# Nested seven-product T1 in the third GLU pass, projection banks seeded by ScalarE, and other stages for the down weights' sums and the k tiles

## The chip, the cores and the metric

The kernel runs on one core of a Trainium2 chip. Its time is the device time of one execution in microseconds; the median of three runs is given.

## The reference

One layer: layer norm, a hedgehog linear attention, a gated linear unit (GLU) on the same normalized input, and their product added to the input. x is 2048 rows of 1024, F is 3584; all data are fp32.

```python
xn = layernorm(x)                       # [2048, 1024]
q, k, v = split(xn @ wqkv)              # three [1024, 1024] products, 32 heads of 32
pq, pk = q @ w_phi, k @ w_phi           # per head
phi_q = concat(softmax(pq), softmax(-pq)); phi_k likewise
s = (phi_q (phi_k^T v)) / (phi_q phi_k^T 1 + 1e-6) @ wo
g = sigmoid(xn @ w_gate) * (xn @ w_up)  # [2048, 3584], here called h
out = x + s * silu(g @ w_down)
```

## The kernel before

**One product.** Every fp32 operand is split into a rounded part hi (a ScalarE cast, L133) and the rest lo (a VectorE subtraction, L134). `mm3` then issues three matmuls into one PSUM bank: hi·hi (L142), hi·lo (L143), lo·hi (L144), each 128x128 by 128x512. Seven block products take the place of eight: the large products go by a Strassen-Winograd scheme over 2x2 blocks, with operand sums made by POOL (GpSimd) and kept in DRAM. The seven are named B11, B21, T2, T3, T4, T1 and B22. B11 and B21 need no sums of weights; T2, T3 and T4 build on B11's result, T1 and B22 on what T2 and T3 left.

**Stages, in TensorE's order** (the list `ops`): the projections V, K, Q of the first half of the rows; GLU pass 0 (B11 and B21 for 14 pairs f of weight tiles); the projections of the second half; GLU pass 1 (T2, T3, T4 for each f); GLU pass 2, the *third pass* (T1 and B22 for each f); the down product (`dsteps`, 112 steps); then the attention's end and the output projection. In a GLU product, a tile f has four banks: gate and up weights (s) by two column halves of the rows (th), bank 2s+th, 12 matmuls each. Pass 1 keeps the banks after B11, T2 and T3 in DRAM (`keep_bank`, m_d), and pass 2 loads them again (`fetch`).

**h in the third pass.** `h_added` adds a bank to the fetched tile on VectorE (L1302), applies the sigmoid on ScalarE for the gate's two banks (L1304), and multiplies on POOL (L1306) for the up's two. `h_out` makes the sums of four h tiles on POOL (L1276 to L1279) and stores seven kinds of h for the down stage.

**Weights.** A ring of eight slots (`w`, `NW = 8`) holds split weights. `prep` makes the next item whenever slots are free: it takes a raw buffer loaded by `glu_load`, casts, subtracts, and gives the buffer back to `raw_free`. `tick` counts steps of the program (four per GLU product); `later(n, f)` runs f after n ticks, and such work is put behind the last matmul issued. All data transfers are issued on the SP queue.

**Sums of weights.** `glu_group` makes the sums of the gate and up weights on POOL in pass 1, for f = 2 to 12 (`FLY`). `wd_sums` makes the sums of the down weights, in 14 sets: four loads of 256 KB, four POOL subtractions of 128x512 (L789 to L792), four stores of 256 KB. In this kernel all 14 sets run in the third pass. `k_steps` and `k_end` handle the k tiles of the attention: nine in the second projections (`EARLY`), the others in pass 1, one each 6.5 ticks; the second `k_end` (transposes L678) falls into the third pass.

**Projections.** `proj_out` evacuates a bank after each product: B11 and B21 by ScalarE copies, T2, T3, T4, T1 and B22 by VectorE additions (L541) of the bank and a tile in SBUF. Products in `opening` (B11, T2, T3, T1) start a new bank.

**The way into the down stage.** `down_prep` loads and splits a weight tile and two h tiles for a later down step; it needs slots from `wfree` and `hfree`. Four slots (16 to 19) go to `wfree` after T1 of f = 12, that is 144 matmuls ahead of the first down product.

Of the kernel before, what the change touches and what calls it, by code (L numbers as in the profile page):

```python
# [18 lines left out]
P = 128  # L19
# [8 lines left out]
HB = 512  # L28
# [21 lines left out]
def hedgehog_glu_kernel(  # L50
# [62 lines left out]
    EARLY = 9  # L113
# [279 lines left out]
    ops += [("glu", p, f, i) for p in (1, 2) for f in range(NJ) for i in PASSES[p]]  # L393
    items = []
    for n, op in enumerate(ops):
        items += [(n, 2), (n, 2)] if op[0] == "proj" else [(n, 1), (n, 1)]
# [8 lines left out]
    raw_free, spare, groups, made_sums = deque(), [], deque((f, s) for f in FLY for s in range(2)), {}  # L405
# [30 lines left out]
    def glu_group():  # L436
# [3 lines left out]
        f, s = groups.popleft()  # L440
        a11, a12, a21, a22, s1 = bs = [raw_free.popleft() for _ in range(5)]
# [17 lines left out]
        if not groups:  # L459
            kept = [b for b in raw_free if not any(b is o for o in spare)]  # L460
            raw_free.clear()
            raw_free.extend(kept)

# [22 lines left out]
    def prep():  # L486
# [7 lines left out]
        if kind == "glu":  # L494
# [9 lines left out]
            glu_load(n + 1)  # L504
        flow["item"] += 1
        flow["made"] += size
        if kind == "proj":
# [19 lines left out]
    def proj_out(c, which, i, u, b, held=None):  # L527
# [255 lines left out]
    def wd_sums(j, b):  # L783
# [16 lines left out]
        later(4, sums)  # L800
        later(7, keep)
# [439 lines left out]
    def fetch(f):  # L1241
        if f == NJ or f in fetched:
            return
        if phase == 1:
            fetched[f] = [None, None, m1[4 * (f % 2):4 * (f % 2) + 4] if f else halves(48, 49)]
            for b, o in enumerate(fetched[f][2]):
                nc.sync.dma_start(o, m_d[0, f, b])
            return
        fetched[f] = {}
        for m in (2, 1):  # L1250
            fetched[f][m] = [uvfree.popleft() for _ in range(4)]
            for b, o in enumerate(fetched[f][m]):
# [71 lines left out]
    def begin_pass(p):  # L1324
# [12 lines left out]
        elif p == 1:  # L1337
            gates_r.items = halves(45, 46)
# [8 lines left out]
        else:  # L1347
            for n in range(NJ):
                queue2(3 + 8 * n if n < 3 else 26 + 13 * (n - 3) // 2, wd_sums, n,
                       halves(*((43, 44), (53, 54))[n % 2 if n > 2 else 0]))  # L1350

    phase = 0
    for n, (kind, c, what, i) in enumerate(ops):
# [3 lines left out]
        if kind == "proj":  # L1357
# [5 lines left out]
            for u in range(4):  # L1363
                if i in opening:
                    pbank[u] = pmm.next()
                us = slice(u * P, (u + 1) * P)
                for k in range(4):
                    mm3(pbank[u], (xo[:, k, 0, us], xo[:, k, 1, us]), pair(ws[k]),
                        i in opening and k == 0, k == 3, skip_group_check=True)
# [26 lines left out]
        phase, f = c, what  # L1396
# [330 lines left out]
```

## Time and profile before

| | |
|---|---|
| median of 3 runs | 2376.79 us (2374.76 to 2378.82) |
| profiled execution: its time, its span | 2374.87 us, 2373.1 us |
| busy share of the span | PE 99%, DVE (VectorE) 68%, ACT (ScalarE) 45%, POOL 40% |
| matrix matmuls L142, L143, L144 | 390, 389, 389 ns each, pipelined |
| third pass, 1308.6 to 1617.0 us | 308.4 us, DMA share 0.92 |
| down stage, 1617.0 to 2160.4 us | 543.4 us, DMA share 0.70 |

A group of instructions is given as line, engine, operation, output <- input, shape, count, then busy time in us and the mean of one in ns, then the engine's idle time just before them and what ended it. A row of windows gives the stretch, its length, the busy us of PE, PEld (weight loads), DVE, ACT and POOL with counts, the granted clock of TensorE, the DMA engines' busy share, and GB/s.

### The profile page before, as it was taken

The numbers are of one execution on the slowest core, as the hardware profiler recorded it, in microseconds if no ns is written. First come the engines' busy times: TensorE is split into PE (matmuls) and PEld (weight loads), VectorE is DVE, ScalarE is ACT, GpSimd is POOL, SyncE is SP. The second block draws the span as 40 slices with busy tenths as digits, with TensorE's granted clock in tenths as the row PEclk, the third lists the DMA queues.
The fourth block names the chain that finished last, engine by engine and source line by source line (L and its number), as shares of the span: only waits on it lengthen the run. The fifth ranks groups of instructions, "written<-read, shape, count | busy, mean of one in ns | idle before, by whom it ended". The sixth has DMA issues, their size and how long they took to land.

```text
span 2373.1 us, 32026 instructions
## 1 busy us (share of the span) xinstructions
PE 2360.2 (99%) x10972; PEld 1967.2 (83%) x10972; DVE 1610.1 (68%) x2103; ACT 1060.4 (45%) x1603; POOL 954.5 (40%) x617
## 2 busy tenths in 40 slices
PE   9999999999999999999999999999999999999999
PEld 8887888888888888888888888888888888888887
DVE  8635776674677947567766533345888998877776
ACT  7333454464333545565555422223443334355553
POOL 0323237711131045445410687853423334324566
PEclk9999999999999999999999999999999999999999
DMA  8799989975687776677756999977676766876665
GB/s 295 259 317 354 373 316 376 388 266 175 201 278 257 269 279 232 229 245 247 250 184 199 344 396 364 355 251 246 208 233 230 239 209 210 287 272 221 205 208 177
DMA packets 287732, 631.45 MB, mean 266 GB/s; under 512 B 36688, under 2 KB 36944, under 8 KB 282960
## 3 DMA queue, kind: packets, MB, share of 16 engines
q1 hardware_dynamic: 287568, 629.40, 76.1%
q8 instruction: 86, 1.41, 0.2%
q14 instruction: 78, 0.64, 0.1%
HBM read 376.31 MB, written 252.97 MB: 265 GB/s over the span
## 4 chain that ended last, share of the span: by engine, by line
PE 90%; DMA 4%; DVE 3%; POOL 1%; issue 1%; ACT 1%; SPq 0%; DVEq 0%; ACTq 0%; POOLq 0%
PE bank L142 28%; PE bank L143 28%; PE bank L144 28%; PE bank L642 1%; PE bank L932 1%; PE bank L908 1%; DMA wf_d<-fc 1%; DVE w L134 1%; DMA qkv_d<-fc 1%; PE bank L1182 1%; PE bank L366 1%; DMA fa<-wf_d 1%; DVE x L134 0%; DMA g_d<-fc 0%; DMA fc<-wo 0%
## 5 line engine op out<-in xcount | busy, mean ns | idle before, releaser
L142 PE MATMUL bank<-x,w 128*128 128x512 f32 x2352 | 915.7, 390 | 1.6 <-DVE fc L1496 1.6
L143 PE MATMUL bank<-x,w 128*128 128x512 f32 x2352 | 915.5, 389 | 0.0
L144 PE MATMUL bank<-x,w 128*128 128x512 f32 x2352 | 914.1, 389 | 0.7 <-DVE w L134 0.7
L134 DVE TENSOR_TENSOR w<-fa,w 128x512 fp32r<-128x512 f32 (+1 forms) x437 | 406.5, 935 | 216.9 <-ACT w L133 201.0
L133 ACT CAST w<-fa 128x512 fp32r<-128x512 f32 (+1 forms) x437 | 298.2, 685 | 552.4 <-PE bank L143 380.2
L142 PEld LDWEIGHTS bank<-x,w 128*128 128x128 f32 x2352 | 441.6, 188 | 92.8 <-DVE fc L1496 2.0
L144 PEld LDWEIGHTS bank<-x,w 128*128 128x128 f32 x2352 | 441.5, 188 | 92.6 <-DVE w L134 1.1
L143 PEld LDWEIGHTS bank<-x,w 128*128 128x128 f32 x2352 | 441.6, 188 | 90.7
L142 PE MATMUL bank<-w,x 128*128 128x512 f32 x708 | 278.2, 393 | 1.8 <-DVE fb L541 1.6
L143 PE MATMUL bank<-w,x 128*128 128x512 f32 x708 | 276.3, 390 | 0.2 <-DVE w L1118 0.2
L144 PE MATMUL bank<-w,x 128*128 128x512 f32 x708 | 276.0, 390 | 0.0
L142 PEld LDWEIGHTS bank<-w,x 128*128 128x128 f32 x708 | 133.0, 188 | 29.9 <-issue 1.6
L144 PEld LDWEIGHTS bank<-w,x 128*128 128x128 f32 x708 | 132.9, 188 | 28.1 <-DVE x L1108 0.3
L143 PEld LDWEIGHTS bank<-w,x 128*128 128x128 f32 x708 | 133.1, 188 | 26.4 <-DVE w L1118 0.6
L864 POOL TENSOR_TENSOR fc<-fc 128x1024 f32<-128x1024 f32 x32 | 81.6, 2549 | 180.1 <-ACT fc L584 129.7
L1261 ACT COPY fc<-bank 128x512 f32<-128x512 f32 x168 | 97.5, 584 | 102.9 <-PE bank L144 67.4
L1302 DVE TENSOR_TENSOR x<-x,bank 128x512 f32<-128x512 f32 x80 | 54.8, 687 | 117.1 <-PE bank L144 108.4
L134 DVE TENSOR_TENSOR x<-fa,x 128x512 fp32r<-128x512 f32 x112 | 112.8, 1007 | 13.7 <-ACT x L133 13.6
L876 POOL TENSOR_TENSOR fc<-fc,sa 128x1024 f32<-128x1024 f32 x32 | 70.0, 2187 | 89.7 <-DVE sa L873 89.7
L133 ACT CAST x<-fa 128x512 fp32r<-128x512 f32 x112 | 69.2, 618 | 47.8 <-DMA fa<-wd_d 27.3
L134 DVE TENSOR_TENSOR p<-fc,p 128x512 fp32r<-128x512 f32 (+1 forms) x65 | 54.1, 843 | 53.1 <-ACT p L133 52.6
L541 DVE TENSOR_TENSOR fc<-fc,bank 128x512 f32<-128x512 f32 x72 | 48.7, 681 | 42.9 <-PE bank L144 29.7
(311 smaller groups left out, 3153.2 us busy)
## 6 DMA issues: line engine op xcount, KB each, us to landing
m_d<-fc SPq DMA_DIRECT2D x168, 256.0 KB, 4.1
fa<-h_d SPq DMA_DIRECT2D x84, 512.0 KB, 4.2
x<-m_d SPq DMA_DIRECT2D x132, 256.0 KB, 5.1
fa<-wf_d SPq DMA_DIRECT2D x32, 1024.0 KB, 6.2
h_d<-fc SPq DMA_DIRECT2D x100, 256.0 KB, 5.1
fc<-e_d SPq DMA_DIRECT2D x48, 512.0 KB, 4.8
fc<-qkv_d SPq DMA_DIRECT2D x80, 256.0 KB, 4.2
fa<-wg_d SPq DMA_DIRECT2D x68, 256.0 KB, 5.1
```

The costliest lines, as they stand in the source:

```text
L133: nc.scalar.copy(o[0], src)
L134: i = nc.vector.tensor_sub(o[1], src, o[0].bitcast(F32))
L142: nc.tensor.matmul(o, a[0], b[0], start=first, stop=False, **kw)
L143: nc.tensor.matmul(o, a[0], b[1], start=False, stop=False, **kw)
L144: last_mm[:] = [nc.tensor.matmul(o, a[1], b[0], start=False, stop=last, **kw).ins]
L366: nc.tensor.matmul(ps[:, gs], r[:, gs], bd[:, 4 * f + g], start=True, stop=True)
L541: last_dve[:] = [nc.vector.tensor_add(y, x, b).ins]
L642: nc.tensor.matmul(kvb[g // 2][:, g % 2 * 256:g % 2 * 256 + 256], v[:, g].rearrange("p a f -> p (a f)"), ph[:, g].rearrange("p a f -> p (a ...
L864: nc.gpsimd.tensor_mul(ez, e, zb)
L876: nc.gpsimd.tensor_mul(e3, e3, r2[:, :, None].to_broadcast([P, 32, DH]))
L1261: nc.scalar.copy(o, banks[b])
L1302: last_dve[:] = [nc.vector.tensor_add(us[b], us[b], banks[b]).ins]
```

## The change

**Nested products.** For f = 2 to 13 in the third pass, T1 is itself made by seven products of halved blocks. `nest(n, f)` makes T1 of f+1 that way (seven products of six matmuls, 42 in place of 48) and B22 of f as before (`plain(q)`, 48 matmuls). The seven go through banks a, b, c, g (4 to 7): B11 into a, copied to b by ScalarE; T2 on top in b, copied to c; T1 into g; B21 on top in a; T3 on top in c, copied to a; T4 on top in a; B22 on top in g. `result` adds a bank to the fetched tile on VectorE (L1473) and copies it by ScalarE into bank q (L1474), where the matmuls of plain(q) then accumulate. `added` copies g to SBUF and adds it to c and to b. Each nest has six weight items: two loaded pairs of tiles are turned by four POOL sums of 128x256 (`nest_load`) into five and a half casts and subtractions. The rows' side (`x_nest_load`, `x_nest_sums`, `x_nest_split`) is made once, ahead of and at the start of the third pass.

**Projections.** Outside the first eight products, T2 and T3 accumulate in B21's bank, seeded by a ScalarE copy of the kept tile, and T2, T3 and T4 are evacuated by ScalarE copies; T1 and B22 stay VectorE additions.

**Down weights' sums.** Seven of the 14 sets move into pass 1 (between the groups of f = 4 to 10, with four raw buffers for eight ticks each), two stay in the third pass, five go to down steps 1 to 25 (`wd_steps`).

**k tiles.** Eleven in the second projections, the others one each 6 ticks, so that both `k_end` fall into pass 1.

**The way into the down stage.** Slots 16 to 19 go to `wfree` after the last nest, 48 matmuls ahead of the end of the pass.

The core of the diff:

```diff
-    EARLY = 9
+    EARLY = 11
     def tick():
             glu_group()
+            nest_load()
-    ops += [("glu", p, f, i) for p in (1, 2) for f in range(NJ) for i in PASSES[p]]
+    ops += [("glu", 1, f, i) for f in range(NJ) for i in PASSES[1]]
+    ops += [("glu", 2, 0, T1), ("glu", 2, 0, B22), ("glu", 2, 1, T1)]
+    ops += [("nest", 2, f, B22) for f in range(1, NJ - 1)] + [("glu", 2, NJ - 1, B22)]
+    WD_B, WD_C = range(7), range(7, 9)
+    for f in FLY:
+        groups.extend((f, s) for s in range(2))
+        if 0 <= f - 4 < len(WD_B):
+            groups.append((WD_B[f - 4], None))
+    def wd_group(j):
+        bs = [raw_free.popleft() for _ in range(4)]
+        wd_sums(j, bs)
...
+        later(8, free)
+    def nest_load():
+        if not nests or len(raw_free) < 6 or ops.index(("glu", 2, 1, T1)) not in wraw:
+            return
+        k = nests.popleft()
+        ra, rb, rc, rd, gate, up = [raw_free.popleft() for _ in range(6)]
+        for s, o in enumerate((ra, rb)):
+            nc.sync.dma_start(o, wg_d[summed.index(T1), k + 1, :, s * HB:(s + 1) * HB])
+        for s, o in enumerate((gate, up)):
+            last_load[:] = [nc.sync.dma_start(o, wg_d[summed.index(B22), k, :, s * HB:(s + 1) * HB]).ins]
+        def sums():
+            nc.gpsimd.tensor_add(rc[:, hi], rb[:, lo], rb[:, hi])
+            nc.gpsimd.tensor_sub(rb[:, lo], ra[:, lo], rb[:, lo])
+            nc.gpsimd.tensor_sub(rc[:, lo], rc[:, hi], ra[:, lo])
+            nc.gpsimd.tensor_sub(rd[:, lo], ra[:, hi], rc[:, lo])
+            nested[k] = rc, ra, gate, rb, rd, up
+        later(4, sums)
     proj_out:
         (B21)
+            if held is None:
+                nc.scalar.copy(b, u1p[u])
+        elif held is None and i in (T2, T3):
+            nc.scalar.copy((u1p if i == T2 else u2p)[u], b)
+        elif held is None and i == T4:
+            y = yp.next()
+            nc.scalar.copy(y, b)
+            store(0, 1, y)
     begin_pass:
-                at += 6.5
+                at += 6
         else:
-            for n in range(NJ):
-                queue2(3 + 8 * n if n < 3 else 26 + 13 * (n - 3) // 2, wd_sums, n, ...)
+            later(3, raw_free.extend, spare)
+            for n, j in enumerate(WD_C):
+                queue2(20 + 8 * n, wd_sums, j, halves(53, 54))
+    def nest(n, f):
+        def result(q, ps):
+            nc.vector.tensor_add(va[q], va[q], ps)
+            nc.scalar.copy(banks[q], ps)
+            if q < 2:
+                nc.scalar.activation(va[q], va[q], AF.Sigmoid)
+        def added(o, n):
+            x = slots[38][:, n]
+            nc.scalar.copy(x, g)
+            nc.vector.tensor_add(o, o, x)
+        product(B11, a, True)
+        nc.scalar.copy(b, a)
+        plain(0)
+        product(T2, b, False)
+        nc.scalar.copy(c, b)
+        product(T1, g, True)
+        product(B21, a, False)
+        result(0, a)
+        plain(1)
+        product(T3, c, False)
+        nc.scalar.copy(a, c)
+        added(c, 0)
+        plain(2)
+        product(T4, a, False)
+        result(2, a)
+        gated(0)
+        product(B22, g, False)
+        added(b, 1)
+        plain(3)
+        result(3, c)
+        result(1, b)
+        gated(1)
     main loop:
+        if kind == "nest":
+            nest(n, f)
+            if f == NJ - 2:
+                wfree.extend(range(16, 20))
+            tick()
+            continue
-        elif phase == 2 and f == NJ - 2 and i == T1:
-            wfree.extend(range(16, 20))
+        elif (phase, f, i) == (2, 1, T1):
+            x_nest_split(T1)
     down stage:
+        if n in wd_late:
+            wd_steps(n)
```

(`tick` and `used` calls inside `nest` are left out here.) TensorE's row at the seam between the two products of one f in the third pass, before; x0 and x2 are the split rows, w the ring of split weights:

```order
L144 MATMUL bank3_104<-x0_4_9231,w_0_94 128x512
L142 MATMUL bank0_101<-x2_5_9285,w_0_94 128x512
L143 MATMUL bank0_101<-x2_5_9285,w_0_94 128x512
L144 MATMUL bank0_101<-x2_5_9285,w_0_94 128x512
L142 MATMUL bank0_101<-x2_5_9285,w_0_94 128x512
```

T1's last bank is followed by B22's first; between two uses of a bank lie 36 matmuls of the others. The same engine after, in the middle of the nests, from T4's last matmul (rows p) on:

```order
L144 MATMUL bank4_105<-p_2_9774,w_0_94 128x512
L142 MATMUL bank7_108<-x0_4_9420,w_0_94 128x512
L143 MATMUL bank7_108<-x0_4_9420,w_0_94 128x512
L144 MATMUL bank7_108<-x0_4_9420,w_0_94 128x512
L142 MATMUL bank7_108<-x0_4_9420,w_0_94 128x512
L143 MATMUL bank7_108<-x0_4_9420,w_0_94 128x512
L144 MATMUL bank7_108<-x0_4_9420,w_0_94 128x512
L142 MATMUL bank3_104<-x6_5_9526,w_0_94 128x512
L143 MATMUL bank3_104<-x6_5_9526,w_0_94 128x512
L142 MATMUL bank4_105<-x1_4_9336,w_0_94 128x512
L143 MATMUL bank4_105<-x1_4_9336,w_0_94 128x512
L144 MATMUL bank4_105<-x1_4_9336,w_0_94 128x512
```

Bank 4 closes with T4 and is opened again by the next nest's B11 (x1) eight matmuls later. ScalarE in the third pass before; fa are raw buffers, x3, x5 and fc hold fetched tiles:

```order
L1304 ACTIVATE x5_3_9410<-x5_3_9410 128x512
L133 CAST w_0_94<-fa_0_97 128x512
L1304 ACTIVATE x3_4_9409<-x3_4_9409 128x512
L133 CAST w_0_94<-fa_0_97 128x512
L1304 ACTIVATE x3_4_9409<-x3_4_9409 128x512
L133 CAST w_0_94<-fa_0_97 128x512
L1304 ACTIVATE fc_0_100<-fc_0_100 128x512
```

It casts and applies sigmoids by turns, and touches no bank. ScalarE after, from the last evacuation of one nest through most of the next; L1492, L1496 and L1507 are the copies to b, c and a:

```order
L1474 COPY bank2_103<-bank4_105 128x512
L1480 COPY p2_2_9775<-bank7_108 128x512
L1492 COPY bank5_106<-bank4_105 128x512
L133 CAST w_0_94<-fa_0_97 128x512 x3
L1496 COPY bank6_107<-bank5_106 128x512
L133 CAST w_0_94<-fa_0_97 128x512
L1474 COPY bank0_101<-bank4_105 128x512
L1476 ACTIVATE x3_4_9582<-x3_4_9582 128x512
L1474 COPY bank1_102<-bank5_106 128x512
L1476 ACTIVATE x3_4_9582<-x3_4_9582 128x512
L1507 COPY bank4_105<-bank6_107 128x512
L1480 COPY p2_2_9775<-bank7_108 128x512
```

Nine copies from or into banks now stand between the casts, three of them (to b, c and a) between two products of the same nest, and the three casts of one group stand ahead of the copy to c.

More of the change, by code (lines that the diff above doesn't have):

```diff
@@ L504, in prep @@
             glu_load(n + 1)
+        if kind == "nest" and what not in nested:
+            return False
         flow["item"] += 1
         flow["made"] += size
+        if kind == "nest":
+            s = len(ready[n])
+            src, cols = nested[what][s], slice(0, 256 if s == 4 else HB)
+            split(cut(pair(w), cols), src[:, cols])
+            release(src)
+            ready[n].append(w)
+            return True
         if kind == "proj":
@@ L799, in wd_sums @@
             nc.sync.dma_start(b, wd_block(i, j))
-        later(4, sums)
-        later(7, keep)
+        return sums, keep
+    def wd_sums(j, b):
+        for n, f in zip((4, 7), wd_parts(j, b)):
+            later(n, f)
     def down_prep():
```

129 lines of the change are left out of this document (108 added, 21 removed).

## The prediction

> **What bounds the kernel now.** I read the page's engines and its chain first, then TensorE's (PE's) waits, then windows by stage.
>
> ```profile
> PE 2360.2 (99%) x10972; PEld 1967.2 (83%) x10972; DVE 1610.1 (68%) x2103; ACT 1060.4 (45%) x1603; POOL 954.5 (40%) x617
> PE 90%; DMA 4%; DVE 3%; POOL 1%; issue 1%; ACT 1%; SPq 0%; DVEq 0%; ACTq 0%; POOLq 0%
> ...
> PE bank L142 <- DVE fb L541: 1.6, 3, 0.8
> PE bank L142 <- DVE fc L1496: 1.6, 1, 1.6
> ...
> PE bank L908 <- DMA fc<-e_d: 1.1, 1, 1.1
> PE bank L678 <- issue: 0.8, 1, 0.8
> ```
>
> PE is busy for 2360 of 2373 us and makes up 90% of the chain; its longest wait is 1.6 us. So the time is a count of matmuls times their spacing, and a saved matmul is worth its spacing as long as what feeds PE keeps pace. The stages (length, then busy PE, PEld, DVE, ACT and POOL, clock, DMA share, GB/s):
>
> ```profile
> 590.80:828.10 237.30, 237.30 (x1081) 197.80 (x1080) 183.12 (x209) 97.48 (x114) 36.79 (x23) 1.00 0.74 249
> 828.10:1308.60 480.50, 480.50 (x2205) 400.92 (x2204) 309.53 (x342) 265.79 (x401) 179.94 (x115) 1.00 0.69 234
> 1308.60:1617.00 308.40, 307.64 (x1366) 254.72 (x1365) 131.88 (x188) 80.64 (x136) 228.57 (x167) 1.00 0.92 335
> 1400.00:1600.00 200.00, 200.00 (x885) 165.58 (x884) 81.39 (x115) 47.96 (x77) 154.63 (x113) 1.00 0.92 334
> 1617.00:1753.00 136.00, 136.00 (x602) 112.61 (x601) 106.79 (x152) 53.02 (x87) 48.06 (x22) 1.00 0.68 231
> 1753.00:2000.00 247.00, 247.00 (x1091) 204.55 (x1090) 224.16 (x330) 98.87 (x160) 88.83 (x39) 1.00 0.68 227
> ```
>
> These are the second projections, pass 1, the third pass, its middle, and two parts of the down stage. PE never rests in them, and the granted clock is 1.00 throughout. In the third pass VectorE (DVE) and ScalarE (ACT) are idle for over half the time; DMA is what is full there (0.92). In the down stage DVE is the second engine: 79%, then 91%.
>
> **The gain.** The middle of the third pass gives the spacing: 200 us / 885 = 0.226 us. A tile of the third pass has 96 matmuls, 48 of T1 and 48 of B22; in a nest T1 has seven products of six, 42. Twelve tiles save 72 matmuls, 72 x 0.226 = 16.3 us, and a tile goes from 21.7 to 90 x 0.226 = 20.3 us, if PE never waits. No other part of the change removes a matmul; all else can only cost, or free a wait that PE has now (the rows above: 1.6 + 0.8 us at most).
>
> **The nests.** The three places where one could wait are priced from these rows: a last matmul with the DVE addition and ACT operation that follow it, ACT and DVE work by kind, POOL's, and the time of loads from issue to landing.
>
> ```profile
> 1426.36 0.39 PE L144 MATMUL bank<-x,w 128*128 128x512 f32 x1
> 1426.79 0.69 DVE L1302 TENSOR_TENSOR fc<-fc,bank 128x512 f32<-128x512 f32 x1 [2.03 <-PE bank L144]
> 1427.51 0.63 ACT L1304 ACTIVATE fc<-fc 128x512 f32<-128x512 f32 x1 [0.28 <-DVE fc L1302]
> ...
> L133 ACT CAST w<-fa 128x512 fp32r<-128x512 f32 x57 | 35.4, 621 | 119.7 <-PE bank L143 97.4 <-issue 6.8 <-PE bank L144 4.2
> L134 DVE TENSOR_TENSOR w<-fa,w 128x512 fp32r<-128x512 f32 x57 | 48.6, 853 | 8.9 <-ACT w L133 8.8
> L1257 ACT COPY bank<-x x52: 578/591/615, 853.4 to 1275.5; 128x512 f32<-128x512 f32 x52
> L789 POOL TENSOR_TENSOR fb<-fb 128x512 f32<-128x512 f32 x8 | 10.4, 1295 | 36.5 <-DMA fb<-w_down 36.5
> L792 POOL TENSOR_TENSOR fc<-fc 128x512 f32<-128x512 f32 x6 | 8.7, 1453 | 0.0
> L1306 POOL TENSOR_TENSOR x<-x 128x512 f32<-128x512 f32 x22 | 31.1, 1419 | 16.2 <-DVE x L1302 16.2
> fa<-wg_d SPq DMA_DIRECT2D x43, 256.0 KB, 5.1
> ```
>
> *Throughput first.* A nest gives ACT six casts less a half (5.5 x 0.62), nine copies (9 x 0.59) and four sigmoids (4 x 0.63): 11.2 us of 20.3. DVE gets 5.5 subtractions (0.85) and ten additions (0.69): 11.6 us. POOL gets four products (1.42), four half-width sums (about 0.7, half of 1.3 to 1.45) and four sums of h (1.4): 14 us. None is full. DMA is relieved: 12 of the 14 sets of down-weight sums leave the stage, each 8 transfers of 256 KB, which is 25 MB of the 103 MB (335 GB/s x 308.4 us) that the stage moves. So only latency in the loop can bite.
>
> *Place 1, T4 to the next B11.* Both use bank a (bank 4), and eight matmuls lie between, so nine spacings, 2.03 us. In that time DVE must start after the last matmul (+0.43, from the first two rows), ACT's copy follows its start by 0.72 and takes 0.59, and some 0.05 passes on release: 1.80 us. It fits by 0.2 us if ACT is free. The copies to b, c and a have twelve matmuls or more to hide them.
>
> *Place 2, the loop through the weights.* A nest may load only when six raw buffers are free. Counted from T4's last matmul: the last cast before it starts at +0.4, behind a sigmoid; DVE's subtraction releases the buffer at +1.9; the load lands 5.1 later, +7.0; three half-width sums on POOL, +9.1; three casts follow, and queued behind the first of them on ACT stand the copy to c, another cast and the seed of bank 0, which is done at +13.6. PE arrives at plain(0) 61 spacings after, +13.8. So the loop closes with 0.2 us to spare, and a nest takes the larger of 20.34 and 20.17 + (landing - 5.1).
>
> *Place 3, the last product of B22*, whose first matmuls need a cast made after T4's fifth: some 0.5 us of slack.
>
> If no place ever waits, the price is 0; if half of the nests lose 1 us in one of them, 6. I take 1.5, nearer to the lower end, since the landing is 5.1 with a DMA share of 0.92 and that share falls.
>
> One rule of the Trainium skill speaks against the change. "TensorE: Matmul & The Clock Gate", section "A second HAM failure mode: psum-queue depth-cycling", says that cycling through banks with small idles between groups makes the clock switch between half and full speed. The traced down stage changes its bank every three matmuls and keeps 1.00, so I add nothing; by the rule the nests' clock would drop, which is a rival below.
>
> **Rows for the nests.** The four sums of two column halves of T1's rows: 8 POOL subtractions, 8 casts and subtractions, four loads of 512 KB near the seam of pass 1 and the third pass. 8 x 0.62 on ACT and 8 x 0.85 on DVE lie beside 20 us of a tile's matmuls. 0 to 2 us (a late first split, as half of the work): I take 0.5.
>
> **Projections.** These rows price them:
>
> ```profile
> L541 DVE TENSOR_TENSOR fc<-fc,bank x72: 628/680/689, 56.8 to 817.7; 128x512 f32<-128x512 f32 x72
> ...
> ACT p L133 <- DMA fc<-wo: 24.7, 8, 8.1
> ```
>
> For each of the five later projections 12 DVE additions (0.68) turn into copies of 0.59 on ACT, and four seeds are added there. PE comes back to a bank after 36 matmuls, 8.1 us, and copy and seed need 0.43 + 2 x 0.59 = 1.6. What could break it is ACT being held: it waited up to 8.1 us for wo's rows in the first projections, and copies now queue behind such a cast: 8.1 + 1.6 - 8.1 = 1.6 us, two or three times. From -1.6 (PE's waits on L541 go) to +4; I take 0.
>
> **Pass 1.** Seven sets put 28 POOL subtractions (1.3 to 1.45 each, 39 us) beside 180 us of 480, and 56 transfers of 256 KB (14.7 MB, at 335 GB/s 44 us) on the SP queue ahead of later loads, with DMA at 0.69. Four raw buffers are away for eight ticks, seven times; casts then run closer behind POOL's sums. Two k tiles more run in the projections. The wait of 0.8 at L678 may move or go. From -0.9 to +3; I take 0.
>
> **Into the down stage.** The first down product's operands could be split from 144 matmuls (32.5 us) ahead, now from 48 (10.8 us). The chain for the first is a load of about 5.1, three casts (1.9) and a last subtraction (0.85), 7.9 us, and a step of 24 matmuls is 5.4 us, above three casts or three subtractions (2.6). So it is ready before, if SP's queue isn't held; late by a landing costs 5. I take 1.5 of 0 to 5.
>
> **Sums in the down stage.** Twenty POOL subtractions (20 x 1.3 to 1.45 = 26 to 29 us) and 40 transfers come within steps 1 to 25, about 135 us, where DVE splits run:
>
> ```profile
> L134 DVE TENSOR_TENSOR w<-fa,w x140: 628/683/2627, 1622.4 to 1999.4; 128x512 fp32r<-128x512 f32 x140
> L134 DVE TENSOR_TENSOR x<-fa,x x69: 627/680/2889, 1624.7 to 1995.2; 128x512 fp32r<-128x512 f32 x69
> ```
>
> The median split takes 0.68, but up to 2.6 or 2.9 us. In the third pass, with POOL busy for 229 of 308 us, the same operation averages 0.85: 57 x 0.17 = 9.7 us lost, so 28 us more of POOL cost 28 x 9.7 / 229 = 1.2 us of DVE time. The other end is that DVE stands still for all of it, 28 us, against its idle 136 - 106.8 = 29.2 us in the first window and 22.8 in the next. Taken: 1 us, of 0 to 8.
>
> The Trainium skill's "SBUF — State Buffer", section "🔬 SBUF: two separate sides", takes that other end: an operation of DVE with both inputs in SBUF and one of GpSimd lock each other out for the whole instruction. By the longest split above (2.89) the trace bears it out for single instructions, by the mean of 0.85 not for the sum.
>
> **The sum.** -16.3 + 1.5 + 0.5 + 0 + 0 + 1.5 + 1 = -11.8 us. From the profiled execution's 2374.87 that is 2363.1; the median of the three runs lies 1.9 us above it, so the forecast is 2365.0. A difference of 0.2%, 4.75 us, is about what a measurement of this kernel can tell from no change: below 2372.0 counts as faster, above 2381.5 as slower.
>
> **Rivals.**
> *The down stage eats the gain.* If POOL's sums hold DVE for their full length, DVE's need in the first window is 106.8 + 28 = 135 of 136 us; the lead with which splits run ahead isn't rebuilt, and in the second window (91%) PE waits. If a fifth to a half of the 28 us reaches PE, 6 to 14 us come back: -11.8 - 1 + 6 to 14 from the median gives 2370 to 2378. For it: the 2.9 us. Against: DVE isn't over full even then. 0.13.
> *Slower: the nest's loop closes through the load.* A transfer of 256 KB takes 0.78 us at 335 GB/s; three more ahead of it in the queue (a fetch of four tiles, or four stores of h) make the landing 7.5 in place of 5.1. Then a nest takes 20.17 + 2.4 = 22.57, 2.2 us over PE's own, and 12 x 2.2 = 26.8: -16.3 + 26.8 + 3 = +13.5, about 2390. It outweighs the gain from a landing of about 6.4 on. For it: 0.2 us of slack, a release, a load, POOL, ACT and DVE in one chain, and in-order ACT with the seed behind the cast. Against: 5.1 is the median in a fuller queue. 0.15.
> *The clock drops in the nests,* by the many short accumulations: at half the rate 12 x 20.3 = 244 us more, 2610. No row shows a clock under 1.00. 0.02.
> *The nests don't save what they should,* since matmuls of six per bank run less tightly: at 0.240 spacing, 1080 x 0.014 = 15 us are lost and the time is unchanged, 2377 to 2380. The down stage's three per bank run at 247 / 1091 = 0.226, which speaks against it. 0.02.
> The forecast keeps 0.68.
>
> **How the numbers follow.** The forecast's own range: gains of PE's present waits (-2.5) and all costs at zero give -16.3 - 2.5 + 1.9 from 2374.87, 2358.0; costs at half their upper ends (the upper ends of 6, 2, 4, 3, 5 and 8 us don't meet), 14, give 2374.5. To hold 0.8 it takes in most of the down rival, to 2377. Faster: 0.67 of the forecast and 0.06 of the down rival, 0.73; the same: the rest of both and the loose spacing, 0.10; slower: the loop, the clock, 0.17.
>
> **What would show it.** Right: records of L142, L143 and L144 fall by 24 each; the third pass lasts about 293 us at a spacing of 0.226; PE has no wait over 0.5 us on an ACT copy or a cast within it; wg_d loads land in about 5 us or less; splits in the down stage stay near a median of 0.68. Wrong: a regular wait of 1 to 2 us per nest on plain(0)'s seed (the loop), waits of bank a on ACT at each T4 (place 1), DVE subtractions at 2 us and waits on w in 1650 to 1900 us (the down stage), or a clock under 1.00.

## The result, and the profile after

The changed kernel takes 2417.57 us (median; 2413.48 to 2420.85) against 2376.48 us: 1.0171 times the time before, 95% interval 1.0151 to 1.0192. That is slower by 41 us, where 12 us less were forecast. The profiled execution's span went from 2373.1 to 2418.3 us. The page of the changed kernel, its engines and its costliest group (count, busy us, mean ns, then the idle time before it):

```profile
PE 2364.4 (98%) x10900; PEld 1961.7 (81%) x10900; DVE 1668.7 (69%) x2099; ACT 1158.1 (48%) x1817; POOL 1019.9 (42%) x673
...
L142 PE MATMUL bank<-x,w 128*128 128x512 f32 x2304 | 900.6, 393 | 43.4 <-ACT fc L1323 19.8
```

The 72 matmuls are gone (10972 to 10900), but TensorE's idle time before L142's matmuls rose from 1.6 to 43.4 us. What it waited for (us in total, times, longest):

```profile
PE bank L142 <- ACT fc L1323: 19.8, 8, 5.8
PE bank L142 <- ACT bank L1474: 10.9, 6, 2.6
PE bank L142 <- DVE fc L1667: 5.8, 1, 5.8
PE bank L142 <- ACT bank L1319: 3.3, 3, 2.8
PE bank L142 <- DVE x L1364: 2.8, 1, 2.8
```

L1323 is `keep_bank`'s copy and L1319 the seed, both of pass 1; L1474 is the seed of plain(q) in the nests, L1364 the addition in `h_added`; L1667 is the evacuation of B21 in the down stage. Windows by stage of the changed kernel: projections and pass 0 (to the last addition of a projection), pass 1 (to the first addition in `h_added`), third pass (to the last of these), the down stage to the first sigmoid there (or its table load), and the rest:

```profile
0.00:831.00 831.00, 826.62 (x3887) 690.93 (x3888) 546.75 (x664) 429.16 (x604) 231.80 (x157) 1.00 0.83 295
831.00:1352.70 521.70, 498.56 (x2247) 411.81 (x2246) 326.07 (x343) 258.83 (x409) 234.21 (x158) 0.99 0.73 249
1352.70:1657.00 304.30, 290.38 (x1239) 235.46 (x1238) 170.05 (x223) 139.92 (x253) 211.17 (x164) 0.98 0.74 250
1657.00:1811.60 154.60, 151.11 (x666) 124.44 (x664) 126.73 (x165) 56.75 (x96) 76.52 (x40) 1.00 0.81 287
1811.60:2418.30 606.70, 597.73 (x2867) 499.10 (x2867) 499.11 (x708) 273.49 (x458) 266.18 (x156) 0.99 0.67 227
```

Cut in the same way, the kernel before has 830.9, 487.6, 298.7, 147.9 and 608.0 us. So the projections cost nothing (+0.1), pass 1 costs 34.1, the third pass 5.6 in place of a gain of 16.3, the start of the down stage 6.7, and the rest gains 1.3: together 45.2.

**The granted clock fell as well.** Two-microsecond windows around one wait in the nests:

```profile
1440.00:1442.00 2.00, 1.94 (x9) 1.09 (x7) 2.00 (x3) 1.03 (x2) 2.00 (x2) 1.00 0.90 289
1442.00:1444.00 2.00, 0.19 (x1) 0.00 (x0) 2.00 (x3) 0.00 (x0) 1.92 (x2) 1.00 0.15 39
1444.00:1446.00 2.00, 1.21 (x4) 0.98 (x5) 1.34 (x3) 1.75 (x4) 1.84 (x3) 0.82 0.95 293
1446.00:1448.00 2.00, 2.00 (x7) 1.52 (x6) 0.96 (x2) 1.23 (x3) 1.24 (x1) 0.50 1.02 360
1448.00:1450.00 2.00, 2.00 (x9) 1.63 (x8) 0.98 (x2) 0.90 (x2) 1.29 (x1) 0.82 0.93 240
```

TensorE stood for 2.6 us, took up work at full clock, and then had half the clock for some 3.4 us (0.7, 2.0 and 0.7 by the last three rows). Over the whole trace, spacings between the starts of matmuls above 0.6 us, less 0.227 each, sum to 50.1 us (6.5 before), and spacings of 0.3 to 0.6 us, where the reduced clock shows, less 0.227 each, to 28.6 us (11.2 before): 43.6 + 17.4 = 61 us lost. Less the 16.3 gained that is 44.7, against a difference of 45.2.

### The profile page after: what moved, and what is told of

It reads as the page before. It is cut to its first block, busy times and chain, and to the rows that moved or that the text cites. A ratio compares the mean times of both kernels' runs of the same rounds, so it can differ in the third digit from the quotient of the medians.

```text
span 2418.3 us, 32136 instructions
## 1 busy us (share of the span) xinstructions
PE 2364.4 (98%) x10900; PEld 1961.7 (81%) x10900; DVE 1668.7 (69%) x2099; ACT 1158.1 (48%) x1817; POOL 1019.9 (42%) x673
## 5 line engine op out<-in xcount | busy, mean ns | idle before, releaser
L142 PE MATMUL bank<-x,w 128*128 128x512 f32 x2304 | 900.6, 393 | 43.4 <-ACT fc L1323 19.8
L143 PE MATMUL bank<-x,w 128*128 128x512 f32 x2304 | 902.9, 392 | 1.1 <-DVE x L134 1.1
L144 PE MATMUL bank<-x,w 128*128 128x512 f32 x2304 | 900.2, 392 | 0.0
L134 DVE TENSOR_TENSOR w<-fa,w 128x512 fp32r<-128x512 f32 (+2 forms) x453 | 449.7, 1000 | 279.8 <-ACT w L133 256.1
L142 PEld LDWEIGHTS bank<-x,w 128*128 128x128 f32 x2304 | 435.9, 189 | 144.0 <-ACT fc L1323 23.2
L144 PEld LDWEIGHTS bank<-x,w 128*128 128x128 f32 x2304 | 435.8, 189 | 91.7 <-DVE w L134 0.4
L143 PEld LDWEIGHTS bank<-x,w 128*128 128x128 f32 x2304 | 435.8, 189 | 90.3 <-DVE x L134 1.5
L133 ACT CAST w<-fa 128x512 fp32r<-128x512 f32 (+2 forms) x453 | 303.2, 677 | 380.7 <-PE bank L143 257.6
L142 PE MATMUL bank<-w,x 128*128 128x512 f32 x708 | 277.8, 393 | 0.4 <-DVE fb L593 0.4
L142 PEld LDWEIGHTS bank<-w,x 128*128 128x128 f32 x708 | 133.1, 188 | 27.6 <-DVE fb L593 1.0
L1323 ACT COPY fc<-bank 128x512 f32<-128x512 f32 x168 | 96.6, 585 | 102.7 <-PE bank L144 52.9
L134 DVE TENSOR_TENSOR x<-fa,x 128x512 fp32r<-128x512 f32 x112 | 118.5, 1059 | 20.9 <-ACT x L133 20.7
L644 ACT ACTIVATE fc<-fc 128x1024 f32<-128x1024 f32 x48 | 50.9, 1060 | 91.9 <-DVE fc L641 78.1
L134 DVE TENSOR_TENSOR p<-fc,p 128x512 fp32r<-128x512 f32 (+1 forms) x67 | 63.5, 955 | 28.8 <-ACT p L133 28.4
L1009 POOL TENSOR_TENSOR fc<-fc 128x512 f32<-128x512 f32 x32 | 49.3, 1539 | 53.8 <-DVE fb L1020 19.9
```

The source lines that it names most:

```text
L133: nc.scalar.copy(o[0], src)
L134: i = nc.vector.tensor_sub(o[1], src, o[0].bitcast(F32))
L142: nc.tensor.matmul(o, a[0], b[0], start=first, stop=False, **kw)
L143: nc.tensor.matmul(o, a[0], b[1], start=False, stop=False, **kw)
L144: last_mm[:] = [nc.tensor.matmul(o, a[1], b[0], start=False, stop=last, **kw).ins]
L644: nc.scalar.activation(e, e, AF.Exp)
```

## The experiments

A run without interval is one profiled execution, read by stage. All are edits of the changed kernel. Single executions whose text of a stage is the same differ: the projections and pass 0 take 828.4 to 836.8 us, pass 1 with its sets 520.0 to 526.1, the third pass with two sets and eight buffers 299.9 to 304.3. Smaller differences in a stage tell nothing. Stages in us, as cut above:

| run | proj., pass 0 | pass 1 | third | to B21's end | rest | span |
|---|---|---|---|---|---|---|
| before | 830.9 | 487.6 | 298.7 | 147.9 | 608.0 | 2373.1 |
| after | 831.0 | 521.7 | 304.3 | 154.6 | 606.7 | 2418.3 |
| sets_p3 | 832.0 | 495.7 | 313.0 | 152.3 | 607.0 | 2400.0 |
| sets_dma_only | 836.8 | 520.0 | 302.5 | 155.0 | 607.2 | 2421.6 |
| hold_p1 | 831.4 | 492.8 | 311.0 | 152.0 | 605.7 | 2392.8 |
| loads_p1 | 832.7 | 511.1 | 313.9 | 152.2 | 606.2 | 2416.1 |
| stores_p1 | 832.7 | 497.2 | 312.2 | 153.3 | 605.9 | 2401.3 |
| idle_p1 | 868.8 | 495.2 | 312.8 | 152.2 | 605.3 | 2434.3 |
| k_13_65 | 832.8 | 520.8 | 300.1 | 151.1 | 607.3 | 2412.2 |
| sets_p0 | 847.1 | 495.6 | 299.9 | 152.6 | 605.8 | 2401.0 |
| no_nest | 828.8 | 529.4 | 294.8 | 147.9 | 607.2 | 2408.1 |
| nest_12raw | 830.7 | 523.6 | 289.1 | 154.4 | 607.1 | 2404.9 |
| down_lead | 834.9 | 526.1 | 303.7 | 152.2 | 606.2 | 2423.1 |
| down_p3 | 828.4 | 524.1 | 312.6 | 146.4 | 606.2 | 2417.6 |
| best1 | 846.3 | 487.4 | 286.4 | 152.0 | 605.9 | 2378.1 |
| best2 | 833.5 | 488.3 | 295.8 | 153.7 | 607.3 | 2378.6 |
| best3 | 831.5 | 488.2 | 300.1 | 156.1 | 604.9 | 2380.7 |
| best4 | 841.6 | 489.4 | 287.0 | 153.0 | 605.2 | 2376.3 |
| best5 | 839.1 | 488.2 | 293.0 | 152.8 | 604.9 | 2378.1 |
| best6 | 831.4 | 488.5 | 293.0 | 153.5 | 605.5 | 2371.8 |

**Pass 1: sets or k tiles?** From the time lines of POOL, ScalarE and VectorE of the changed kernel around the longest wait (TensorE stands from 1133.7 to 1139.4), then ScalarE's waits in the whole pass:

```profile
1122.41 1.61 POOL L458 TENSOR_TENSOR fa<-fb,fb 128x512 f32<-128x512 f32 x1 [8.18 <-DMA fb<-w_gu]
...
1126.78 0.62 ACT L133 CAST w<-fa 128x512 fp32r<-128x512 f32 x1 [2.68 <-POOL fa L460]
...
1127.43 1.22 DVE L134 TENSOR_TENSOR w<-fa,w 128x512 fp32r<-128x512 f32 x1 [3.36 <-ACT w L133]
...
1134.21 1.74 DVE L641 TENSOR_TENSOR fc<-stk,fc 128x512 f32<-128x512 f32 x1
...
1129.30 0.57 ACT L1323 COPY fc<-bank 128x512 f32<-128x512 f32 x1
1136.03 1.28 ACT L644 ACT_TABLE_LOAD   x1 [6.16 <-DVE fc L641]
1137.33 1.06 ACT L644 ACTIVATE fc<-fc 128x1024 f32<-128x1024 f32 x1
...
1138.80 1.06 ACT L1323 COPY fc<-bank 128x512 f32<-128x512 f32 x2
```

```profile
ACT fc L644 <- DVE fc L641: 41.8, 9, 7.7
...
ACT w L133 <- POOL fa L460: 15.5, 4, 8.1
```

The copies that free TensorE's banks stand in ScalarE's queue behind the exponential of a k tile (L644), which waits for VectorE, which in turn had waited for a cast held by late sums of gate and up weights. All nine of TensorE's waits in pass 1 that are longer than 0.7 us stand behind such an exponential. What kept VectorE is not the same each time: at three, with 11.2 of the 22.6 us, it had waited 3.2 to 8.1 us for a cast as here; at two it had waited 6.9 and 7.6 us for a transfer (a load of qkv_d, a store of zb_d); at the other four it had been at work without a wait above 0.6 us. First the sets were moved out of pass 1 (sets_p3), and apart from that their POOL subtractions left out:

```diff
-    WD_B, WD_C = range(7), range(7, 9)
+    WD_B, WD_C = range(0), range(9)          # sets_p3
```


> The seven sets of down-weight sums of pass 1 run in the third pass instead (nine there); all else as changed. From the last projection addition to the first addition of the third pass the kernel before takes 487.6 us and the changed one 521.7. Theory 1 (the sets cause pass 1's loss, by buffers, transfers or POOL): back to 488 to 492, and the third pass gets worse by what 28 more POOL subtractions and 56 transfers do to the nests: 0 to 15 us above 304. Theory 2 (k tiles each 6 ticks instead of 6.5 cause it): pass 1 stays at 515 to 522. Whole run 2387 to 2400 by theory 1, 2415 or more by theory 2.


```diff
-        wd_sums(j, bs)
+        later(7, wd_parts(j, bs)[1])         # sets_dma_only
```


> In pass 1 the seven sets of down weights are loaded and stored as before, with the same buffers and times, but their 28 POOL subtractions are left out (so the stored blocks are not the sums). If POOL's work and the VectorE operations that it lengthens cause the loss of 34 us in pass 1, pass 1 falls from 521.7 to 488 to 497. If the raw buffers and transfers taken from the groups of gate and up weights cause it, it stays at 512 to 522, and ScalarE's casts go on waiting for late POOL sums.

Without the sets pass 1 takes 495.7 us, somewhat above the 488 to 492 expected: they cost 26 of the 34. Without their subtractions it stays at 520.0, so it is not POOL's work there. Buffers away without transfers, and the loads or stores alone, all on sets_p3's placing:

```diff
         bs = [raw_free.popleft() for _ in range(4)]
-        wd_sums(j, bs)                       # hold_p1: no more than this
+        # loads_p1:  4 x nc.sync.dma_start(b, wd_block(i, j))
+        # stores_p1: later(7, keep_idle)  4 x nc.sync.dma_start(idle_d[j, k], b)
+        # idle_p1:   4 + 4 copies of w_down's blocks from DRAM to DRAM
```


> The seven sets run in the third pass (nine there), but in pass 1 four raw buffers are still taken away for eight ticks at each of the seven places, with no load, sum or store. Pass 1 takes 521.7 us with the sets and 495.7 without. If the buffers that are away are the cause, it takes 510 to 522; if the 56 transfers on the SP queue are, 494 to 500. The rest as in the run with nine sets in the third pass: third pass about 313.

> As hold_p1 (nine sets in the third pass, four raw buffers away for eight ticks at seven places of pass 1), and the 28 loads of the sets into these buffers are issued in pass 1, with no sums and no stores. Pass 1: 492.8 us with the buffers away alone, 520 with loads and stores. If the loads' places on the SP queue (each may wait there for its buffer, with all later transfers behind it) are the cause, 508 to 520; if the stores are, 493 to 498.

> As hold_p1, and the 28 stores of the sets are issued from the held buffers in pass 1 at their ticks, to a place that nobody reads, with no loads and no sums. If the stores keep the buffers and so the loads of gate and up weights behind them, pass 1 takes 505 to 520; if not, 493 to 498. If loads and stores share the 27 us, both runs lie between.

> Nine sets in the third pass as in the run sets_p3; in pass 1 the four raw buffers are taken away as in hold_p1, and at the same ticks 56 transfers of 256 KB run from DRAM to DRAM, which use no buffer and wait for nothing. Pass 1: 521.7 us with the sets, 492.8 with the buffers away alone. If the traffic and the places on the SP queue are the cause, 510 to 522. If it is the chain load, sum, store through shared buffers, for whose end later loads wait on SP, 492 to 500.

Pass 1 in hold_p1 and in loads_p1, what TensorE waited for there, and in loads_p1 also two of the waits of the SP queue, for the loads of down weights (L480) and of gate and up weights (L455):

```profile
831.40:1324.20 492.80, 490.13 (x2241) 408.71 (x2240) 311.37 (x343) 261.60 (x409) 192.08 (x130) 1.00 0.70 233
...
PE bank L142 <- ACT fc L1322: 2.7, 1, 2.7
```

```profile
832.70:1343.80 511.10, 496.50 (x2245) 411.33 (x2244) 312.54 (x343) 260.01 (x409) 191.45 (x130) 0.99 0.72 240
...
PE bank L142 <- ACT fc L1324: 10.5, 3, 4.7
PE bank L142 <- ACT bank L1320: 4.0, 3, 2.5
...
SPq L455 <- DMA fa<-w_down: 14.4, 7, 3.1
...
SPq L480 <- DMA fa<-w_down: 10.5, 6, 3.4
```

The buffers alone cost nothing that shows (492.8). The 28 loads add 18.3 us, the 28 stores 4.4, which such single runs hardly tell from nothing, both together with the sums 28.9. It is not the bytes: as stores, the same bytes cost a quarter of that, and the loads of gate and up weights land hardly later (medians of 3.6 us into fa and 3.9 into fb in loads_p1, 3.5 and 3.4 in hold_p1). It is the loads' place in line: the loads of down weights waited on the SP queue for 29.8 us in 24 waits, and the loads of gate and up weights that stand behind them were issued later in TensorE's order of matmuls than in hold_p1, by 18 matmuls (4 us; median of the 50 loads from the first set to the last). In stores_p1 the median is 2 matmuls, in the changed kernel 50. idle_p1, which was to show traffic without buffers, says nothing on this, since nothing tied its copies to pass 1 and they ran between 24 and 82 us (where they cost 37 us).

The k tiles, with the sets in place; in this run and in best1 thirteen tiles of the projections come 5.5 ticks apart, closer than a tile is needed in its buffer, so their features are partly overwritten, with the same instructions:

```diff
-    EARLY = 11
+    EARLY = 13
-                at += 6
+                at += 6.5
```


> Thirteen k tiles in the second projections and the others in pass 1 one each 6.5 ticks; the seven sets stay in pass 1. If the raw buffers of the sets cause 26 of the 34 us, and the denser k tiles the other 8, pass 1 falls from 521.7 to 510 to 515, no further, and the projections stay at 831. If the k tiles make the sets hurt (one alone would not), pass 1 falls to 488 to 500.

It stays at 520.8, which neither branch expected: with the sets there, the placing of the k tiles is not what decides. Without the sets it is worth the rest: sets_p0 with eleven tiles ahead and 6 ticks has 495.6, best1 and best2 with thirteen and 6.5 ticks 487.4 and 488.3. No run changes the ticks alone, so the share of the two tiles fewer in pass 1 isn't shown. Put into pass 0, the seven sets cost 16 us there:

```diff
+            for n, j in enumerate(WD_B):     # begin_pass(0)
+                queue2(18 + 8 * n, wd_sums, j, halves(43, 44))
```


> The seven sets of pass 1 run in pass 0 instead, in two tiles that are idle there, so no raw buffer of the weights is taken. If buffers and not the transfers or POOL's work are the cause, pass 1 goes to 495 (as with the sets in the third pass), the third pass stays at 300 to 306, and projections and pass 0 stay at 831 to 834 although DMA has a share of 0.85 there. If 56 transfers hurt wherever they are put, projections and pass 0 lose 5 us or more. Run about 2392.

**The nests.** In the changed kernel's third pass, ScalarE's waits, the time of the weights' loads, and from the time lines of VectorE, SP, POOL and ScalarE in the nest whose wait the clock's windows show (T4's last matmul starts at 1427.39):

```profile
ACT w L133 <- POOL fa L501: 31.5, 8, 6.3
...
fa<-wg_d SPq DMA_DIRECT2D x41, 256.0 KB, 3.7
```

```profile
1429.02 1.78 DVE L134 TENSOR_TENSOR w<-fa,w 128x512 fp32r<-128x512 f32 x1
...
1430.83 0.32 SPq L493 DMA_DIRECT2D fa<-wg_d  x1
...
1436.05 0.74 POOL L499 TENSOR_TENSOR fa<-fa 128x256 f32<-128x256 f32 x1 [1.50 <-DMA fa<-wg_d]
...
1438.34 1.66 ACT L133 CAST w<-fa 128x512 fp32r<-128x512 f32 x3 [6.27 <-POOL fa L501]
...
1438.99 3.96 DVE L134 TENSOR_TENSOR w<-fa,w 128x512 fp32r<-128x512 f32 x3 [1.87 <-ACT w L133]
1442.87 0.69 DVE L1481 TENSOR_TENSOR bank<-bank,p 128x512 f32<-128x512 f32 x1
1443.46 0.67 DVE L1473 TENSOR_TENSOR fc<-fc,bank 128x512 f32<-128x512 f32 x1
...
1444.17 0.57 ACT L1474 COPY bank<-bank 128x512 f32<-128x512 f32 x1 [3.14 <-DVE fc L1473]
```

The chain is the one of the prediction's place 2: the subtraction that frees a buffer, the load, POOL's sums, three casts, three subtractions, the two additions, the seed of bank 0. All six of TensorE's waits on L1474 end with this seed. Two runs, one without nests and one in which a nest need not wait for the buffers of the one before:

```diff
-    ops += [("glu", 2, 0, T1), ...] + [("nest", 2, f, B22) ...]
+    ops += [("glu", 2, f, i) for f in range(NJ) for i in PASSES[2]]        # no_nest
-        if groups or not any(o is b for b in spare):
+        if groups or (phase == 2 and nests) or not any(o is b for b in spare):  # nest_12raw
```


> T1 of all tiles by the plain 48 matmuls as before, all other parts of the change kept. The 72 matmuls come back (+16.3 us), and what the nests lose goes. If the nests lose 22 us by their own loop (waits on the seed of plain(0) and the lower clock after them), the third pass takes about 299 us as before (304 with nests) and the run about 2412. If the third pass loses by other parts of the change (late k tiles, row sums at the seam), it stays at 304 or more plus 16.

> The four spare raw buffers stay in the pool while nests remain, so 12 half tiles instead of 8 after their first use, and the load of a nest need not wait for the release by the last cast of the nest before. If the loop release, load, POOL, cast, seed is what makes every second nest wait 2 us, the waits on L1474 go and the third pass falls from 304.3 to 280 to 286, the run by 18 to 24 us to about 2394 to 2400. If POOL and VectorE work side by side in the nest is the cause (three subtractions of 1.3 us instead of 0.68), the waits stay and it remains at 300 to 304.

TensorE's waits in the third pass of nest_12raw:

```profile
PE bank L142 <- ACT bank L1474: 2.2, 2, 2.0
PE bank L142 <- DVE x L1364: 1.5, 1, 1.5
```

With four more buffers the third pass falls from 304.3 to 289.1 us (280 to 286 expected), though POOL does the same work and VectorE is even busy for longer (180.3 us, 170.1 in the changed kernel); the waits on the seed fall from 10.9 to 2.2 us. Without nests it takes 294.8. So the loop through the weights' buffers made 15.2 of the 21.9 us by which the changed kernel's third pass misses the full gain (298.7 - 16.3 = 282.4).

**The down stage.** The five sets moved away, or slots given earlier in the last nest:

```diff
-    WD_B, WD_C = range(7), range(7, 9)
+    WD_B, WD_C = range(7), range(7, 14)      # down_p3
+            if f == NJ - 2: hfree.append(...); wfree.extend(...)  # down_lead, in nest()
```


> The five sets of the down stage run in the third pass (seven there); the seven of pass 1 stay. From the last addition of the third pass to the first sigmoid of the down stage the changed kernel takes 154.6 us, 147.9 without nests although the five sets are there. If sums beside the splits eat the time in which VectorE would build up its lead after a late start, it falls to 148 to 150. If the late start alone does it, it stays at 152 to 155. The third pass gets worse by 0 to 9 us.

> In the last nest the slots of its rows and of its weights are given to the down stage one by one as its products are done, not all at its end; all else as changed. If the short lead into the down stage causes the stall of 6 us at the end of B21 there (147.9 us from the last addition of the third pass to the first sigmoid of the down stage before, 154.6 changed), it falls to 148 to 151. If the five sets of sums in the down stage cause it, it stays at 154. The run without nests, with these sets and 147.9, speaks for the first.

The window up to B21's end in down_p3, then VectorE's weight splits there in the changed kernel and in no_nest:

```profile
1665.10:1811.40 146.30, 146.30 (x648) 121.12 (x647) 115.81 (x165) 58.34 (x96) 51.11 (x24) 1.00 0.71 246
```

```profile
L134 DVE TENSOR_TENSOR w<-fa,w 128x512 fp32r<-128x512 f32 x55 | 55.3, 1021 | 14.0 <-ACT w L133 14.0
```

```profile
L134 DVE TENSOR_TENSOR w<-fa,w 128x512 fp32r<-128x512 f32 x54 | 43.8, 817 | 26.7 <-ACT w L133 26.7
```

With the late start but no set in the down stage TensorE never waits (146.3 of 146.3): the sums are the cause, and the late start none that shows. no_nest's text leaves the five sets in the down stage, but all 20 of their subtractions were issued earlier, in the third pass (POOL's L848 on fb from 1417.5 us on), and it gives the slots early, as the kernel before does. So its 147.9 doesn't tell the two apart, and doesn't say what the two expectations above make of it. The cost does not go by the number of sums: runs with 16 subtractions in this window take 151.1 to 155.0 us, those with 8 152.8 (best5) and 156.1 (best3). down_lead's 152.2 lies among them, between what its two branches expected. The same 165 VectorE instructions take 126.7 us in place of 115.8 in down_p3. TensorE's wait of 5.8 us on L1667 lies across the end of the window (1809.2 to 1815.0): the sigmoid that it needs comes late, and stands in ScalarE's queue behind an exponential (L644, from 1809.5 on), as the copies in pass 1 do.

**A version with the three causes out of the way.** best1 to best6 have nest_12raw's buffers and 6.5 ticks, and place the 14 sets differently; from best2 on the k tiles of the projections come 6 ticks apart. best1 and best2 have down_lead's slots. In best3 some sets share tiles with other work, so that a part of the sums isn't the reference's.

| | best1 | best2 | best3 | best4 | best5 | best6 |
|---|---|---|---|---|---|---|
| pass 0 / projections / third / down | 7/0/2/5 | 0/0/9/5 | 0/1/10/3 | 3/0/6/5 | 3/0/8/3 | 0/0/9/5, ending earlier |

> The nests with 12 raw buffers, the seven sets in pass 0, thirteen k tiles in the projections and 6.5 ticks, and slots for the down stage in the last nest. If the three causes add up: projections and pass 0 831, pass 1 488, third pass 284 to 290, to the first sigmoid of the down stage 148 to 151, rest 607: 2358 to 2367 for the span, under the 2373 of the kernel before. If a cause is wrong, its stage shows it.

> As the run best1, but the seven sets in the third pass (nine there, in two tiles that the weights don't use), and the thirteen k tiles of the projections one each 6 ticks. If pass 0's loss of 15 us came from the sets: projections and pass 0 831 to 833, pass 1 488. If with 12 raw buffers the nests can stand the sets, the third pass takes 286 to 292; if the transfers hold up the loads as in the run with nine sets and 8 buffers, 295 to 303. Then 152 and 606: 2363 to 2371, or 2372 to 2382; the kernel before takes 2373 in span.

> The nests with 12 raw buffers; ten sets in the third pass from its tick 13 on, one in the second projections before the sums of weights there, three in the down stage; thirteen k tiles in the projections, 6.5 ticks in pass 1; slots for the down stage given at the end of the last nest, as in the changed kernel. If the casts of down operands in the last nest caused the wait of 5.5 us in best2, the third pass takes 287 to 291 (295.8 there); with three sets in the down stage it takes 148 to 152 to the first sigmoid. Then 832 + 488 + 289 + 150 + 606 = 2365 in span, 2362 to 2369, faster than the kernel before by 0.2 to 0.45%. If the sets in the third pass hold up the nests, 2372 to 2378.

> The nests with 12 raw buffers; the 14 sets: three early in pass 0 (its first three cost nothing in sets_p0), six in the third pass, five in the down stage; thirteen k tiles in the projections, 6.5 ticks. Projections and pass 0 831 to 833, pass 1 488, third pass 286 to 290 if the late sets made best2 and best3 wait for the down stage's h, 295 to 300 if not; then 152 to 154 and 606. 2363 to 2369, under the 2373 of before by 0.2 to 0.4%; or 2372 to 2378.

> As best4 with eight sets in the third pass and three in the down stage. If the sums in the down stage cost by their number, 149 to 151 us to the first sigmoid there in place of 153; the third pass 0 to 4 us longer than in best4. 2363 to 2370.

> The nests with 12 raw buffers; nine sets in the third pass, one each seven ticks from its tick 14 and with shorter steps, so that the last ends some 25 ticks before the down stage instead of eight; none in passes 0 and 1, five in the down stage; thirteen k tiles in the projections, 6.5 ticks. Projections and pass 0 831 to 833 (839 to 842 with sets in pass 0), pass 1 488, third pass 287 to 291 if the late sets cost best2 its wait, then 152 to 154 and 606: 2365 to 2371 in span, under the 2373 of before by 0.1 to 0.4%. If the sets hold up the nests wherever they stand in the third pass, 2375 to 2380.

```diff
-                queue2(20 + 8 * n, wd_sums, j, halves(53, 54))
+                queue2(14 + 7 * n, wd_sums, j, halves(53, 54), (3, 5))   # best6
```

To the kernel before: best2 1.0005 (0.9995 to 1.0015), best3 1.0041 (1.0027 to 1.0055), best4 1.0000 (0.9991 to 1.0009), best5 1.0026 (1.0017 to 1.0036), best6 0.9995 (0.9986 to 1.0004). The causes add up: the 41 us are gone. But none is faster than before, best3 and best5 are slower by 0.3 to 0.4%, and no span fell into the range that its better branch expected (2358 to 2371 us in all; 2371.8 to 2380.7 measured). With few sets beside them the nests run at 286.4 and 287.0 us, 12 less than before; what they gain goes back to the sets, which have no place left that costs nothing: 8 to 16 us in pass 0, 6 to 13 more in the third pass if nine or ten run there, some 5 in the down stage. Why three early sets cost pass 0 and the projections 8 to 11 us in best4 and best5 is open. In the kernel before, all 14 run in the third pass, beside matmuls that had slack for them.

## Why the prediction was wrong

**The gain** was right in size: 72 matmuls fewer, and a third pass of 286.4 us where little disturbs it, against 298.7 - 16.3 = 282.4.

**The projections** (taken 0) cost 0.1 us, less than single executions differ by: right, and ScalarE's additional copies there did no harm.

**Pass 1** is the term that failed most: taken 0, of -0.9 to +3, it was +34.1. I priced POOL's 39 us and the bytes at the DMA share, and named the transfers' place on the SP queue ahead of later loads without a price for it. The runs show that the bytes and POOL's work are not the cause and the loads are (18 us alone), and that 8 more go to the placing of the k tiles. No rival held this mechanism. What I should have followed is the chain behind it: late load, late sum, cast held, VectorE late, and behind the exponential that waits for VectorE the copies that free TensorE's banks. The traces show this whole chain for half of the waiting; what made VectorE late in the rest stays open.

**Place 1** was right: no wait on T4's bank appears. **Place 2** was found, with its 0.2 us of slack, and sized wrongly: 1.5 of 0 to 6, where the third pass lost 21.9 (304.3 against 282.4): 10.9 in waits on the seed, 2.8 in a wait for the rows, 8.4 at reduced clock. Four more buffers brought back 15.2 of it. A slack of 0.2 us in a loop that five engines close is no slack; any of its parts may be longer. The slower rival named this loop, but by the landing of the load, from 6.4 us on; loads landed in 3.7. It was the parts before and behind it, VectorE's subtractions above all. In the nest above, the one that frees the buffer took 1.78 us, where one had been priced at 0.85, and ended 3.4 us after T4's last matmul, not 1.9; the load took 5.2, as counted; POOL's third sum ended at +10.9, not +9.1; the three subtractions took 3.96 us, beside POOL's work; the seed was done at +17.4, not +13.6.

**Rows for the nests** (0.5, of 0 to 2) were too low as well: at the start of the third pass TensorE waited 2.8 us for an addition (L1364) behind splits of these rows on VectorE (1.1 and 1.5 us, from 1357.3 and 1360.2 on), and 1.6 us at reduced clock followed. In no_nest, without the rows, this wait is 0.6.

**Sums in the down stage** (1, of 0 to 8) cost 6.7 us against the kernel before and 8.2 against down_p3: the upper end of the bounds, and nearer to the rival's mechanism than to mine. VectorE lost 10.9 us to 16 subtractions, 25.4 us of POOL (76.5 less 51.1). The Trainium skill's "SBUF — State Buffer", section "🔬 SBUF: two separate sides", has the two engines lock each other out; four tenths of POOL's time are nearer to that than my 1.2 us for 28, an average from a stage with a third as many splits in a microsecond (57 in 308 us there, 81 in 155 here). **Into the down stage** (1.5) cost nothing that shows.

**The clock** was looked for in the wrong place. It did not fall for many short accumulations; it fell after waits. The rule that I weighed had the matmuls slow down in the nests as such, and they do not: in best1, with one wait of 2.0 us left in the third pass, spacings of 0.3 to 0.6 us cost 0.5 us there (8.4 in the changed kernel). Of the 61 us lost, 17 are matmuls at reduced clock.

## What to carry to other kernels

Work moved to a stage that never waits has to be followed through every queue that it joins: a transfer can hold up those behind it at a DMA share of 0.72, and an exponential or a cast that waits holds up the copies that free the banks. When a hand count of a loop leaves 1% of slack, count the loop as late, and give it another buffer before anything else. In this kernel, with TensorE at 98 to 99%, waits cost some 40% more than they last, through the clock (17.4 on 43.6 us).

## What the runs showed of the hardware

In the changed kernel, 8 of the 14 waits of 1.7 to 6 us from pass 1 to B21's end (spacings between starts, less 0.227) were followed within 12 us by 7 to 13 matmuls spaced by about 0.42 us, which cost 1.4 to 2.8 us each time. The shortest such waits were 2.1 us; three of 2.2, 2.9 and 3.0 us had no such matmuls behind them, so length alone does not decide. The trace's clock records have 0.50 in eight stretches there, six of 3.4 us and two of 6.8, 34.1 us together, half of which fits the 17.4 us lost; the six began 0.3 to 1.5 us after work was taken up again, the two within the waits of 5.9. The Trainium skill's "TensorE: Matmul & The Clock Gate", section "HAM oscillation — how this bites in real kernels", speaks of idle gaps above some 3.4 us; here the clock fell after shorter ones too.

VectorE's additions with one operand in a bank took 0.69 us in all stages and kernels (673 to 690 ns for L1364); its subtractions of the same size with both operands in SBUF (L134, changed kernel) took 0.68 us where no POOL operation ran at the same time (300 of them) and 1.27 on average, up to 2.89, where one did (288).
